# Transform writes issued from the scalar queue, a down projection of 512 and 128 columns, and a new order of all steps

## The chip, the cores and the metric

The kernel runs on one core of one Trainium2 chip. The core has TensorE (PE, matmuls), VectorE (DVE), ScalarE (ACT), GpSimd (POOL) and SyncE (SP, which here only issues DMAs). The metric is the device time of one execution in microseconds; several executions are made, and their median is compared.

## The reference

Two branches work on one layer-normed input of 2048 positions and 640 channels, and are added to the raw input:

```python
xn = layernorm(A_q)                              # over the 640 channels
ks = sum over 4 taps of shift_k * shifted A_k     # a short causal convolution
kv = ks * A_v
y  = irfft(rfft(kv, 4096) * rfft(ssm_k, 4096))[:2048]   # a long causal convolution, per channel
A  = xn * (y + kv * ssm_D)
B  = (sigmoid(xn @ w_gate) * (xn @ w_up)) @ w_down      # 640 -> 1728 -> 640
out = A_q + A + B
```

All tensors are bf16.

## The kernel before

The 2048 positions lie on 128 partitions with 16 blocks (b) each, so x and xn are tiles of 128 x 16 x 640. Branch B runs in four row groups t of four blocks. For each of 13 pieces fc of 128 hidden columns, `gate_mm` and `up_mm` (lines 295 and 302) make five matmuls of 512 columns each into a PSUM tile, ScalarE takes the sigmoid (`gate_ev`, line 298) and VectorE the product (`up_ev`, line 305); the last 64 columns of both share one product (`both_mm`, line 308). Then the down projection (`down_mm`, line 329) makes for each block bb two halves of 320 output columns, 14 matmuls each, in two parts of seven; only the last block of all is cut into 512 and 128. `down_ev` (line 338) adds a half to x on VectorE.

Branch A works in five chunks c of 128 channels. VectorE makes kv out of four taps in 16 operations (`kv_op`, line 356) and turns the long kernel around (`h_turn`, line 350). The long convolution is a transform in two stages, each a set of matmuls. `st1_mm` (line 386, step a) makes eight pairs of matmuls per chunk; `st1_ev` (step A) casts each pair out of PSUM into a tile t1, of which there are two, so that a tile holds two casts; `wr1` (line 404, step w, four per chunk) writes a tile of 512 KB to DRAM (d1), and `rd2` (line 412, step r) reads it back with the axes turned, for `st2_mm` (line 420, step b). After the product in frequency space (`prod`, step p), the inverse goes the same way: `inv1_mm` (line 445, step c, numbered y from 0 to 9), casts (`inv1_ev`, step C), `wr2` (line 468, step W, one or two DMAs by y), `rdb` (line 478, step R), `inv2_mm` (line 489, step d), and VectorE multiplies by xn and adds to x (step q).

PSUM is held by two pools: psC, two buffers of two banks, for the transform's first three matmul stages, and psG, four buffers of one bank, for the products, the down projection and the second inverse stage.

Casts are done by ScalarE, or by VectorE where the order has the letters F, J or I in place of B, C or A. In the kernel before every load, write and store of DRAM is issued by SP, but for three pieces of x at the start and the last store, which ScalarE issues. The normed rows are turned by DMA transposes (`xn_turn`, line 270, step e), also on SP.

The order is written out by hand as a string of letters, `ORDER` (line 671). Each letter takes the next step of its chain (`step`, line 562); chains m (early loads) and o (stores, line 342) are taken in the permuted sequence of `TURNS`. A letter fixes the place of its step on its own engine's queue; between engines only data and buffers order the work.

```python
    for k in "".join(ORDER.split()):
        fn, args = next(left[{"F": "B", "J": "C", "I": "A", "Y": "E"}.get(k, k)])
        fn(*args, **({"copy": dve_copy} if k in "FJIY" else {}))
```

Of the kernel before, what the change touches and what calls it, by code (L numbers as in the profile page):

```python
# [11 lines left out]
F32 = mybir.dt.float32  # L12
U16 = mybir.dt.uint16
ACT = mybir.ActivationFunctionType
ALU = mybir.AluOpType

S = 2048
DM = 640
FF = 1728
P = 128  # L20
NB = S // P
NC = DM // P
NFC = 14
# [42 lines left out]
def kernel(  # L66
# [14 lines left out]
    nc = tc.nc  # L81
# [19 lines left out]
    psG = ctx.enter_context(tc.tile_pool(name="psG", bufs=4, space=bass.MemoryType.PSUM))  # L101
# [14 lines left out]
    x = res.tile([P, NB, DM], BF16, name="x")  # L116
# [4 lines left out]
    wd = res.tile([P, NFC, DM], BF16, name="wd")  # L121
    hT = res.tile([P, NFC, 512], BF16, name="hT")
# [9 lines left out]
    sync = nc.sync  # L132
# [189 lines left out]

    pds = {}

    def cols(t, bb, half):
        m = 4 * P if (t, bb) == (3, 3) else DM // 2
        return slice(m, DM) if half else slice(0, m)

    def down_mm(t, bb, half, part):
        es = cols(t, bb, half)  # L330
        if part == 0:
            pds[bb, half] = psG.tile([P, es.stop - es.start], F32, name="pd", tag="g")
        pd = pds[bb, half]
        for fc in range(7 * part, 7 * part + 7):
            nc.tensor.matmul(pd[:, :], lhsT=hT[:, fc, bb * P:(bb + 1) * P], rhs=wd[:, fc, es],  # L335
                             start=(fc == 0), stop=(fc == NFC - 1))

    def down_ev(t, bb, half):
        es = cols(t, bb, half)
        nc.vector.tensor_tensor(x[:, 4 * t + bb, es], pds[bb, half][:, :], x[:, 4 * t + bb, es], ALU.add)  # L340

    def store(b0, b1, lo, hi):
        (nc.scalar if b1 == NB and hi == DM else sync).dma_start(outr[:, b0:b1, lo:hi], x[:, b0:b1, lo:hi])
# [60 lines left out]
    def wr1(c, k):  # L404
        h, part = divmod(k, 2)
        d = chunks[c]
        sync.dma_start(d["d1"][:, h, 8 * part:8 * part + 8, :], d[k].rearrange("p b s c -> p b (s c)"))

    groups = {}
    xz = cv.tile([P, 3, 3, 8, P], BF16, name="xz")  # L410
# [57 lines left out]
    def wr2(y):  # L468
        c, y2 = divmod(y, 2)
        d = chunks[c]  # L470
        if 2 * y % 3 < 2:
            sync.dma_start(d["d2"][16 * y2:16 * y2 + 16].rearrange("r p c -> p r c"), d["ao", y])
            return
        for n in range(2):
            lo = 16 * y2 + 8 - 8 * n
            sync.dma_start(d["d2"][lo:lo + 8].rearrange("r p c -> p r c"), d["ao", y][:, 8 * n:8 * n + 8, :])

    def rdb(c, n):

# [82 lines left out]
    def step(k, fn, *args):  # L562
        chains[k].append((fn, args))

    for t in range(4):
        for fc in range(0 if t else 2, 13):
            step("g", gate_mm, t, fc)
            step("s", gate_ev, t, fc)
            step("g", up_mm, t, fc)
            step("u", up_ev, t, fc)  # L570
        step("g", both_mm, t)
        step("s", both_ev, t)
        step("u", both_mul, t)
        firsts = [(0, 0, 0), (0, 1, 0), (0, 0, 1), (0, 1, 1)]
        for bb, e, part in firsts + [(k // 2, k % 2, n) for k in range(2, 8) for n in range(2)]:
            step("g", down_mm, t, bb, e, part)
            if part:
                step("u", down_ev, t, bb, e)

    def hs(c):  # L580
        return [(load_h, c)]
# [33 lines left out]
    for c in range(NC):  # L615
# [6 lines left out]
        for n in range(4):  # L622
            step("w", wr1, c, n)
# [7 lines left out]
        for y in (2 * c, 2 * c + 1):  # L631
            step("c", inv1_mm, y)
            for n in range(2):
                step("C", inv1_ev, y, n)
            step("W", wr2, y)
# [23 lines left out]
        for i in range(4):  # L659
            step("e", xn_turn, g, i)  # L660

    for b in range(0, 12, 2):
        step("o", store, b, b + 2, 0, 4 * P)
    for b in (0, 4, 8):
        step("o", store, b, b + 4, 4 * P, DM)
    for b in range(12, NB - 1):
        step("o", store, b, b + 1, 0, DM)
    step("o", store, NB - 1, NB, 0, 4 * P)
    step("o", store, NB - 1, NB, 4 * P, DM)

    ORDER = """
    mgmLggmmmssugmLuggsmZgmusmmgggmgmuLkHHLgsuksmkggsgmmmuusPlllmmggguklTkkkskkmugsgkumkgsgkmugggsumgKgn
    ekktDauAgakgguIgggLHkeauaggekAuugmDLLkwkeImuguTaaAkkmAgggkHuLwsaaPAgAgggkkkkakuKamkkkwsuggsghwkkAAsK
    aatAugVAuwkkggsHHkarasgukgAAasuggaDwkAAggKTKVsbkkuskkkwBlkggkFKaaAVugkskkpggrAktuusbgkwFBsguhpmuwaAa
    AHDgglsllaanpkkVwuAgsAggreakugpIwagkLkkekgAuuckkTkggCCaAggbBBggarwKkkkukkAKggtHeuubFrBegLuugpbFgBgaa
    kukkpkAAsggVWgkawakskApuugghHaAwDLrrwgspsIaAKugguLVcJCsggpubFpBkggWsbuggpsBuBaAgsakAPnggkspppuucCCgg
    sgrbrkHkglRskkwWBBruugdpbrkgspuBBlgsqdqwcCJqgugsRbBFWggbBBeeuggdkapqlrruqquaAAggldpwqaaAAqegpgagappg
    gIApcuggRJCuuuwebFBwggbuWBppgdquBpgdrrcJsCggqqRbWuFBsppprggsbBguBgsrducqqqdqggRCCbrppBggFubsgguppdBB
    ssqpqcWCdpgrugqqCsqbBFRguugbBBggdssppcgpqdugpqrqCCWusbFBppgWgsguugRcJsguCgsuggggqdduuqqqgguRddqqqgqq
    ggWRRgguuoddogoooqoqqudqdoggoqqoqqooouogguo  # L680
    """
    TURNS = {"m": [18, 21, 0, 5, 1, 10, 2, 7, 4, 14, 9, 6, 15, 12, 13, 11, 8, 17, 16, 20, 23, 22, 25, 24, 26, 19, 3],
        "o": [2, 0, 5, 3, 1, 4, 7, 6, 8, 9, 11, 10, 12, 13]}
    left = {k: iter([v[i] for i in TURNS.get(k, range(len(v)))]) for k, v in chains.items()}
    for k in "".join(ORDER.split()):
        fn, args = next(left[{"F": "B", "J": "C", "I": "A", "Y": "E"}.get(k, k)])
# [32 lines left out]
```

## Time and profile before

| what | value |
|---|---|
| median of 3 runs | 235.99 us (235.92 to 236.65) |
| the profiled execution, its own time | 236.99 us |
| its span in the profile | 234.9 us |
| DMA packets and bytes | 97760, 56.07 MB, mean 239 GB/s |
| DMA by queue | SP's 55.35 MB, ScalarE's 0.36 MB |
| landing of wr1's writes (d<-t), median | 5.7 us |
| landing of rd2's reads (t<-d), median | 6.0 us |

The profile comes from one execution. In a row of the timeline stand the start and the duration in us, the engine, the line of the kernel, the operation with its output and input, the count, and in brackets how long the engine stood idle before it and what released it. Durations of matmuls overlap, since they are pipelined; the pace is read from one start to the next. In a row of a stretch stand for each engine its busy time and its instructions.

### The profile page before, as it was taken

To read this page: it belongs to the slowest core of one execution; us is meant where nothing else is said; L and a number is where in the kernel's file an instruction comes from. 1 tells how busy PE (TensorE), PEld (TensorE's weight loads), DVE (VectorE), ACT (ScalarE), POOL (GpSimd) and SP (SyncE) were. 2 spreads that over 40 slices of the span, in tenths; PEclk is the share of its full clock that TensorE was granted. 3 is DMA by queue.
4 is the path that set the end of the run, shared out by engine and by line. 5 is a ranking of instruction groups with operands and counts; after the bars stand their busy time and mean duration, and the time that the engine had idled before them with its cause. 6 is when DMAs were issued, how large, how long until landed. Compare 5 with 4: busy or idle time off the path is not lost.

```text
span 234.9 us, 5606 instructions
## 1 busy us (share of the span) xinstructions
PE 227.9 (97%) x2281; PEld 121.9 (52%) x2281; DVE 203.0 (86%) x332; ACT 133.7 (57%) x193; POOL 13.1 (6%) x27
## 2 busy tenths in 40 slices
PE   7999999999999999999999999999899989999994
PEld 2854445665444444666444435476554444447772
DVE  4634899878989999999999999996999999995864
ACT  2477432279766587667687768563466656851000
POOL 5201300101100000000012000000000000000000
PEclk9999999999999999999999999999999999999999
DMA  6997999899998998999997998969999678583485
GB/s 174 325 264 158 293 316 252 168 267 209 314 301 204 257 318 275 213 252 180 290 308 180 305 288 192 307 125 279 317 243 265 184 180 226 139 247 104 140 309 178
DMA packets 97760, 56.07 MB, mean 239 GB/s; under 512 B 55943, under 2 KB 91975, under 8 KB 97607
## 3 DMA queue, kind: packets, MB, share of 16 engines
q1 hardware_dynamic: 97158, 55.35, 90.7%
q10 hardware_dynamic: 576, 0.36, 0.8%
q8 instruction: 18, 0.29, 0.6%
q14 instruction: 8, 0.06, 0.1%
HBM read 35.39 MB, written 18.35 MB: 229 GB/s over the span
## 4 chain that ended last, share of the span: by engine, by line
PE 42%; DVE 9%; DMA 5%; SPq 3%; issue 2%; ACT 1%; DVEq 0%
PE pu L291 11%; PE pd L335 11%; PE pg L291 10%; PE psb L495 3%; DMA d<-t 3%; DMA t<-d 2%; PE ps L427 2%; DVE hT L306 2%; PE psa L456 2%; SPq L271 2%; DVE xz L442 2%; DVE xz L440 1%; PE pg L312 1%; PE ps L395 1%; PE ps L393 1%
## 5 line engine op out<-in xcount | busy, mean ns | idle before, releaser
L291 PEld LDWEIGHTS <-w 128*128 128x128 bf16 x500 | 47.0, 98 | 58.4 <-issue 4.6
L335 PE MATMUL pd<-wd,hT 128*128 128x320 bf16 (+2 forms) x448 | 65.5, 299 | 0.0
L291 PE MATMUL pg<-xnT,w 128*128 128x512 bf16 x250 | 62.1, 379 | 0.3 <-ACT xn L223 0.3
L291 PE MATMUL pu<-xnT,w 128*128 128x512 bf16 x250 | 62.3, 380 | 0.0
L335 PEld LDWEIGHTS <-hT 128*128 128x128 bf16 x448 | 42.3, 98 | 21.3 <-issue 2.0
L254 ACT CAST t<-ps 128x1024 bf16<-128x1024 f32 x35 | 34.4, 1013 | 17.1 <-PE ps L395 11.5
L300 ACT ACTIVATE sig<-pg 128x512 bf16<-128x512 f32 x52 | 30.8, 600 | 23.1 <-PE pg L291 18.5
L306 DVE TENSOR_TENSOR hT<-sig,pu 128x512 bf16<-128x512 bf16 x52 | 34.5, 680 | 10.5 <-PE pu L291 5.7
L254 ACT CAST xz<-ps 128x1024 bf16<-128x1024 f32 x29 | 28.4, 1014 | 13.3 <-PE ps L427 13.2
L442 DVE TENSOR_TENSOR xz<-xz 128x2048 bf16<-128x2048 bf16 x20 | 24.4, 1220 | 0.3
L374 DVE TENSOR_TENSOR acc<-acc,tmp 128x1024 bf16<-128x1024 bf16 x30 | 20.7, 690 | 0.5
L372 DVE TENSOR_TENSOR tmp<-kx,sc 128x1024 bf16<-128x1024 bf16 x30 | 20.6, 686 | 0.4
L340 DVE TENSOR_TENSOR x<-pd,x 128x320 bf16<-128x320 f32 (+2 forms) x32 | 15.1, 484 | 5.0 <-PE pd L335 4.6
L500 DVE TENSOR_TENSOR yx<-psb,xn 128x512 bf16<-128x512 f32 x20 | 13.8, 690 | 2.4 <-PE psb L495 1.3
L395 PE MATMUL ps<-kvh,S1t 128*128 128x512 bf16 x40 | 15.5, 388 | 0.0
L393 PE MATMUL ps<-kvh,S1t 128*128 128x512 bf16 x40 | 15.1, 379 | 0.0
L254 ACT CAST ao<-psa 128x1024 bf16<-128x1024 f32 x12 | 11.8, 1014 | 5.5 <-PE psa L456 5.4
L440 DVE STREAM_SHUFFLE xz<-xz 128x512 f32<-128x512 f32 x20 | 14.5, 724 | 0.0
L257 DVE CAST xz<-ps 128x1024 bf16<-128x1024 f32 x11 | 13.4, 1219 | 0.3 <-PE ps L427 0.2
L495 PEld LDWEIGHTS <-TBt 128*128 128x128 bf16 x160 | 10.1, 98 | 2.9 <-issue 0.8
L223 ACT ACTIVATE xn<-x 128x640 bf16<-128x640 bf16 x12 | 8.8, 735 | 4.7 <-DMA x<-in_A_q_dram 4.7
L354 DVE STREAM_TRANSPOSE kvh<-hn 128x512 f32<-128x512 f32 x10 | 10.8, 1093 | 0.2 <-DMA hn<-in_A_ssm_k_dram 0.2
(54 smaller groups left out, 158.6 us busy)
## 6 DMA issues: line engine op xcount, KB each, us to landing
d<-t SPq DMA_DIRECT2D x20, 512.0 KB, 5.7
t<-d SPq DMA_DIRECT2D x20, 512.0 KB, 6.0
bi<-d SPq DMA_DIRECT2D x8, 512.0 KB, 5.2
d<-ao SPq DMA_DIRECT2D x6, 512.0 KB, 4.1
kx<-in_A_k_dram SPq DMA_DIRECT2D x10, 256.0 KB, 6.0
hn<-in_A_ssm_k_dram SPq DMA_DIRECT2D x20, 128.0 KB, 5.2
kvh<-in_A_v_dram SPq DMA_DIRECT2D x10, 256.0 KB, 6.2
x<-in_A_q_dram SPq DMA_DIRECT2D x3, 640.0 KB, 4.8
```

The lines of the kernel that those rows point to most:

```text
L254: nc.scalar.copy(out=out, in_=in_)
L291: nc.tensor.matmul(pg[:, :], lhsT=w[:, c, u * UP + fc * P:u * UP + (fc + 1) * P], rhs=xnT[:, :, c, :], start=(c == 0), stop=(c == NC - 1))
L300: nc.scalar.activation(sig[fc][:, :], pgs[0, fc][:, :], ACT.Sigmoid)
L306: nc.vector.tensor_tensor(hT[:, fc, :], sig[fc][:, :], pgs[1, fc][:, :], ALU.mult)
L335: nc.tensor.matmul(pd[:, :], lhsT=hT[:, fc, bb * P:(bb + 1) * P], rhs=wd[:, fc, es], start=(fc == 0), stop=(fc == NFC - 1))
L372: nc.vector.tensor_tensor(d["tmp"][:, :, :], kx[:, lo + 3 - m:hi + 3 - m, :], sb(m), ALU.mult)
L374: nc.vector.tensor_tensor(d["acc"][:, :, :], d["acc"][:, :, :], d["tmp"][:, :, :], ALU.add)
L393: nc.tensor.matmul(ps[:, 0, :, :], lhsT=S1[:, h, :], rhs=cin[c]["kvh"][:, 0, 4 * n4:4 * n4 + 4, :], start=True, stop=True)
L395: nc.tensor.matmul(ps[:, 1, :, :], lhsT=S1[:, h, :], rhs=hp[:, 2 * n4:2 * n4 + 2, :, :], start=True, stop=True)
L440: nc.vector.stream_shuffle(z[:, 2, :, :].bitcast(F32), z[:, 1, :, :].bitcast(F32), swap)
L442: nc.vector.tensor_tensor(z[:, 1:3, :, :], z[:, 0:1, :, :].to_broadcast((P, 2, 8, P)), z[:, 1:3, :, :], ALU.mult)
L495: nc.tensor.matmul(ps[:, i, :], lhsT=TB[:, h, 4 * m + i, :], rhs=bi[:, h, 4 * (m % 2) + i, :], start=(h == 0), stop=(h == 1))
```

## The change

- `wr1` and `wr2` issue their DMAs from ScalarE's queue in place of SP's.
- The down projection of a block makes 14 matmuls of 512 columns (`down_mm`), and its last 128 columns follow in a function of their own (`rest_mm`), with the rests of four blocks side by side in one PSUM tile; one VectorE addition (`rest_ev`) adds them to x. In the last row group the rests are kept as three and one.
- The stores of the rows 12 to 14, each of 640 columns, are cut into 512 columns and a joint piece of 128.
- `ORDER` and `TURNS` are new throughout.

```diff
--- before.py
+++ after.py
@@ -322,22 +322,27 @@
 
     pds = {}
 
-    def cols(t, bb, half):
-        m = 4 * P if (t, bb) == (3, 3) else DM // 2
-        return slice(m, DM) if half else slice(0, m)
-
-    def down_mm(t, bb, half, part):
-        es = cols(t, bb, half)
+    def down_mm(t, bb, part):
         if part == 0:
-            pds[bb, half] = psG.tile([P, es.stop - es.start], F32, name="pd", tag="g")
-        pd = pds[bb, half]
+            pds[bb] = psG.tile([P, 4 * P], F32, name="pd", tag="g")
         for fc in range(7 * part, 7 * part + 7):
-            nc.tensor.matmul(pd[:, :], lhsT=hT[:, fc, bb * P:(bb + 1) * P], rhs=wd[:, fc, es],
+            nc.tensor.matmul(pds[bb][:, :], lhsT=hT[:, fc, bb * P:(bb + 1) * P], rhs=wd[:, fc, 0:4 * P],
                              start=(fc == 0), stop=(fc == NFC - 1))
 
-    def down_ev(t, bb, half):
-        es = cols(t, bb, half)
-        nc.vector.tensor_tensor(x[:, 4 * t + bb, es], pds[bb, half][:, :], x[:, 4 * t + bb, es], ALU.add)
+    def down_ev(t, bb):
+        b = 4 * t + bb
+        nc.vector.tensor_tensor(x[:, b, 0:4 * P], pds[bb][:, :], x[:, b, 0:4 * P], ALU.add)
+
+    def rest_mm(t, bb, b0):
+        if bb == b0:
+            pds[t, b0] = psG.tile([P, 4, P], F32, name="pr", tag="g")
+        for fc in range(NFC):
+            nc.tensor.matmul(pds[t, b0][:, bb, :], lhsT=hT[:, fc, bb * P:(bb + 1) * P], rhs=wd[:, fc, 4 * P:DM],
+                             start=(fc == 0), stop=(fc == NFC - 1))
+
+    def rest_ev(t, b0, b1):
+        xs = x[:, 4 * t + b0:4 * t + b1, 4 * P:DM]
+        nc.vector.tensor_tensor(xs, pds[t, b0][:, b0:b1, :], xs, ALU.add)
 
     def store(b0, b1, lo, hi):
         (nc.scalar if b1 == NB and hi == DM else sync).dma_start(outr[:, b0:b1, lo:hi], x[:, b0:b1, lo:hi])
@@ -404,7 +409,7 @@
     def wr1(c, k):
         h, part = divmod(k, 2)
         d = chunks[c]
-        sync.dma_start(d["d1"][:, h, 8 * part:8 * part + 8, :], d[k].rearrange("p b s c -> p b (s c)"))
+        nc.scalar.dma_start(d["d1"][:, h, 8 * part:8 * part + 8, :], d[k].rearrange("p b s c -> p b (s c)"))
 
     groups = {}
     xz = cv.tile([P, 3, 3, 8, P], BF16, name="xz")
@@ -469,11 +474,11 @@
         c, y2 = divmod(y, 2)
         d = chunks[c]
         if 2 * y % 3 < 2:
-            sync.dma_start(d["d2"][16 * y2:16 * y2 + 16].rearrange("r p c -> p r c"), d["ao", y])
+            nc.scalar.dma_start(d["d2"][16 * y2:16 * y2 + 16].rearrange("r p c -> p r c"), d["ao", y])
             return
         for n in range(2):
             lo = 16 * y2 + 8 - 8 * n
-            sync.dma_start(d["d2"][lo:lo + 8].rearrange("r p c -> p r c"), d["ao", y][:, 8 * n:8 * n + 8, :])
+            nc.scalar.dma_start(d["d2"][lo:lo + 8].rearrange("r p c -> p r c"), d["ao", y][:, 8 * n:8 * n + 8, :])
 
     def rdb(c, n):
 
@@ -571,11 +576,19 @@
         step("g", both_mm, t)
         step("s", both_ev, t)
         step("u", both_mul, t)
-        firsts = [(0, 0, 0), (0, 1, 0), (0, 0, 1), (0, 1, 1)]
-        for bb, e, part in firsts + [(k // 2, k % 2, n) for k in range(2, 8) for n in range(2)]:
-            step("g", down_mm, t, bb, e, part)
+        for bb, part in ((0, 0), (1, 0), (0, 1), (1, 1), (2, 0), (2, 1)):
+            step("g", down_mm, t, bb, part)
             if part:
-                step("u", down_ev, t, bb, e)
+                step("u", down_ev, t, bb)
+        last = [(0, 3), (3, 4)] if t == 3 else [(0, 4)]
+        for b0, b1 in last:
+            if b1 == 4:
+                step("g", down_mm, t, 3, 0)
+                step("g", down_mm, t, 3, 1)
+                step("u", down_ev, t, 3)
+            for bb in range(b0, b1):
+                step("g", rest_mm, t, bb, b0)
+            step("u", rest_ev, t, b0, b1)
 
     def hs(c):
         return [(load_h, c)]
@@ -659,28 +672,27 @@
         for i in range(4):
             step("e", xn_turn, g, i)
 
-    for b in range(0, 12, 2):
+    for b in range(0, 14, 2):
         step("o", store, b, b + 2, 0, 4 * P)
-    for b in (0, 4, 8):
-        step("o", store, b, b + 4, 4 * P, DM)
-    for b in range(12, NB - 1):
-        step("o", store, b, b + 1, 0, DM)
+    step("o", store, 14, 15, 0, 4 * P)
+    for b in (0, 4, 8, 12):
+        step("o", store, b, min(b + 4, 15), 4 * P, DM)
     step("o", store, NB - 1, NB, 0, 4 * P)
     step("o", store, NB - 1, NB, 4 * P, DM)
 
     ORDER = """
-    mgmLggmmmssugmLuggsmZgmusmmgggmgmuLkHHLgsuksmkggsgmmmuusPlllmmggguklTkkkskkmugsgkumkgsgkmugggsumgKgn
-    ekktDauAgakgguIgggLHkeauaggekAuugmDLLkwkeImuguTaaAkkmAgggkHuLwsaaPAgAgggkkkkakuKamkkkwsuggsghwkkAAsK
-    aatAugVAuwkkggsHHkarasgukgAAasuggaDwkAAggKTKVsbkkuskkkwBlkggkFKaaAVugkskkpggrAktuusbgkwFBsguhpmuwaAa
-    AHDgglsllaanpkkVwuAgsAggreakugpIwagkLkkekgAuuckkTkggCCaAggbBBggarwKkkkukkAKggtHeuubFrBegLuugpbFgBgaa
-    kukkpkAAsggVWgkawakskApuugghHaAwDLrrwgspsIaAKugguLVcJCsggpubFpBkggWsbuggpsBuBaAgsakAPnggkspppuucCCgg
-    sgrbrkHkglRskkwWBBruugdpbrkgspuBBlgsqdqwcCJqgugsRbBFWggbBBeeuggdkapqlrruqquaAAggldpwqaaAAqegpgagappg
-    gIApcuggRJCuuuwebFBwggbuWBppgdquBpgdrrcJsCggqqRbWuFBsppprggsbBguBgsrducqqqdqggRCCbrppBggFubsgguppdBB
-    ssqpqcWCdpgrugqqCsqbBFRguugbBBggdssppcgpqdugpqrqCCWusbFBppgWgsguugRcJsguCgsuggggqdduuqqqgguRddqqqgqq
-    ggWRRgguuoddogoooqoqqudqdoggoqqoqqooouogguo
+    mLmgmggssmumggsgmLLmmmumugmmsHmmgggusugsLgmugmHgggZkkmPskmuggsgsusgkkkukmggglmlksemTmDauukkknAllsuka
+    AkkktggwkgggeeaHamguueIAkkkuTgaLAmakkggwKILguakKLaHkDkmwgguggLPAAkkVkgswggsgkkkhuusatKKAaggkkAkmkkks
+    waaluTkAAuwgrsrkggsHguaAgDakkkgkKAHVgausnkkawgmullAAsgbkktBFwuksggahaIsggpAwuukkkbBpBgsgusVaagglkkgu
+    rAAwskkpkgHasALeuueaKgapAAHggwkcCJgbDBuFkgaarATAVrgaeukgwALkkekbBKpkkFkwggubBFgtLggruaKKhAaAwgggpsaa
+    ppppkuWuksgVrAAwgLagPsAukkaAHllkwgggcsVgusgCCugHWbsrukDgBsgkkFbBBggusaanAkkgukggkAkppspcuRJsgruCgWbr
+    suFgpBpggswbgBuudprBdRgqqqscCCulkggskqpWlbgFuBeedbrrBkFgaadqppgAAepaIawAgcuCCpgqupgauRWIaAegwbrqqgdd
+    gFBRbgupprBqqgBpgcsCqqguuwgpCWgbFgdBpqsprsbugBBrgsqudRcCqggJbupBFpggWbssrBBggrupqpddscRuCqqqqCWggupb
+    BggFpppssubBguBgdrcCdCsqqggppbqRRFgsguBppggscuudgWgsCJWqqqguodqsuRggdqqqdqRgguuguogodqqqdgogoddqqgoo
+    qqoqqugoooouoguo
     """
-    TURNS = {"m": [18, 21, 0, 5, 1, 10, 2, 7, 4, 14, 9, 6, 15, 12, 13, 11, 8, 17, 16, 20, 23, 22, 25, 24, 26, 19, 3],
-        "o": [2, 0, 5, 3, 1, 4, 7, 6, 8, 9, 11, 10, 12, 13]}
+    TURNS = {"m": [21, 1, 18, 7, 0, 4, 6, 5, 9, 14, 2, 10, 13, 12, 15, 8, 20, 11, 17, 16, 22, 23, 25, 24, 26, 19, 3],
+        "o": [0, 4, 5, 1, 2, 9, 8, 7, 6, 10, 11, 3, 12, 13]}
     left = {k: iter([v[i] for i in TURNS.get(k, range(len(v)))]) for k, v in chains.items()}
     for k in "".join(ORDER.split()):
         fn, args = next(left[{"F": "B", "J": "C", "I": "A", "Y": "E"}.get(k, k)])
```

## The prediction

> **What bounds the kernel now.** I read the page's head first, then busy time by stretches, then TensorE's instructions in order of time, and last the waits and the chain of waits. The head and the stretches:
>
> ```profile
> span 234.9 us, 5606 instructions
> PE 227.9 (97%) x2281; PEld 121.9 (52%) x2281; DVE 203.0 (86%) x332; ACT 133.7 (57%) x193; POOL 13.1 (6%) x27
> ```
>
> ```profile
> 80.00:100.00 20.00, 20.00 (x167) 10.14 (x166) 19.73 (x31) 13.72 (x20) 0.48 (x1) 1.00 1.01 259
> 100.00:120.00 20.00, 19.91 (x210) 11.20 (x209) 19.66 (x33) 14.41 (x20) 0.00 (x0) 1.00 1.10 245
> 120.00:140.00 20.00, 20.00 (x212) 8.40 (x210) 19.97 (x30) 16.18 (x26) 2.46 (x3) 1.00 0.97 277
> 160.00:170.00 10.00, 9.23 (x122) 5.83 (x121) 7.71 (x12) 3.83 (x4) 0.00 (x0) 1.00 1.09 294
> 180.00:193.00 13.00, 12.08 (x202) 5.91 (x192) 12.65 (x22) 9.07 (x12) 0.00 (x0) 1.00 0.75 200
> ```
>
> The columns are PE, weight load, DVE, ACT and POOL busy, clock, DMA share, GB/s. TensorE and VectorE are both full from 80 us on, with one hole at 160 to 170, and the clock is full. So the kernel sits at TensorE's own work, VectorE right behind it, and an order can win only TensorE's gaps. These I take from starts in TensorE's timeline, since the printed ends overlap the next start:
>
> ```profile
> 20.33 1.24 PE L291 MATMUL pu<-xnT,w 128*128 128x512 bf16 x5
> 21.86 1.25 PE L291 MATMUL pg<-xnT,w 128*128 128x512 bf16 x5 [0.29 <-ACT xn L223]
> ...
> 162.85 2.06 PE L335 MATMUL pd<-wd,hT 128*128 128x320 bf16 x14
> 165.68 0.65 PE L456 MATMUL psa<-xz,SMt 32*32 32x512 bf16 x32 [0.77 <-DVE t L257]
> ...
> 187.64 1.03 PE L291 MATMUL pg<-xnT,w 128*128 128x512 bf16 x4
> 188.59 0.44 PE L427 MATMUL ps<-t,FWt 32*32 32x256 bf16 x32
> 188.97 1.25 PE L291 MATMUL pu<-xnT,w 128*128 128x512 bf16 x5
> 190.05 1.24 PE L291 MATMUL pg<-xnT,w 128*128 128x512 bf16 x5
> 191.13 0.61 PE L495 MATMUL psb<-bi,TBt 128*128 128x128 bf16 x8
> 192.66 0.65 PE L456 MATMUL psa<-xz,SMt 32*32 32x512 bf16 x32 [0.92 <-DVE xz L440]
> ```
>
> Five matmuls of 512 columns take 1.08 us (188.97 to 190.05), 0.216 each. So the first gap is 21.86 - 20.33 - 1.08 = 0.45 us. Fourteen of 320 columns take 1.90 (rows further below), so the second is 165.68 - 162.85 - 1.90 = 0.93. A matmul of 128 columns takes 0.056 (16 in 1.06 us, below, against 8 in 0.61), so eight take 0.44 and the third is 1.53 - 0.44 = 1.09. A step of 32-row matmuls starts some 0.09 late even where nothing waits (188.59 - 187.64 - 4 x 0.216), so 0.84 and 1.00 of the last two can go: **2.29 us in all**.
>
> The chain of waits and the list of waits name the causes:
>
> ```profile
> 155.64 0.46 ACT t L254
> ...
> 156.55 1.03 ACT t L254
> 157.59 6.62 DMA d<-t
> ...
> 164.41 1.24 DVE t L257
> ```
>
> ```profile
> DVE t L257 <- DMA d<-t: 2.3, 1, 2.3
> PEld L291 <- DMA w<-in_B_w_gate_dram: 0.8, 1, 0.8
> ```
>
> The reader is to see that the write of line 407 leaves SP right after its cast ends (157.58), and lands 6.62 us later. VectorE stands 2.3 us for its buffer (there are two tiles t1), TensorE follows at 165.68, and VectorE, which has no slack after that, hands the rest on as the gap at 192.66. The gap at 21.86 is put down to ScalarE; the weight load's wait names the real one, a piece of w.
>
> **The down projection: nothing on TensorE, little on VectorE.**
>
> ```profile
> 212.50 3.97 PE L335 MATMUL pd<-wd,hT 128*128 128x320 bf16 x28
> 216.30 1.06 PE L495 MATMUL psb<-bi,TBt 128*128 128x128 bf16 x16
> ...
> 227.48 3.97 PE L335 MATMUL pd<-wd,hT 128*128 128x512 bf16 x28
> ```
>
> Two halves of 320 take 3.80 us to the next start (0.136 each). The last row is the one block that already runs 14 of 512 and 14 of 128 columns: the same 3.97. So 0 us, in 16 blocks. On VectorE:
>
> ```profile
> L340 DVE TENSOR_TENSOR x<-pd,x 128x320 bf16<-128x320 f32 x30 | 14.1, 483 | 4.8 <-PE pd L335 4.6
> L340 DVE TENSOR_TENSOR x<-pd,x 128x512 bf16<-128x512 f32 x1 | 0.7, 691 | 0.1
> L257 DVE CAST xz<-ps 128x1024 bf16<-128x1024 f32 x11 | 13.4, 1219 | 0.3 <-PE ps L427 0.2
> ```
>
> Eight evictions of 483 become five of 512 elements at 691: 3.86 against 3.46, 0.41 less per row group, 1.2 in the three that lie before 193 us. The new order turns one more cast over to VectorE before its last inverse stage 1 (21 against 20): 1.22 back. VectorE's sum up to there is unchanged.
>
> **The order around t1.** The late write is chunk 4's second of four (wr1 4,1). Between the matmuls of step a whose cast it follows (4,3) and those whose cast needs its buffer (4,6) the old order has four down parts of 0.95, one inverse block of 0.44 and two a's of 0.43: 5.1 us of TensorE work. The new one has four parts of 7 x 0.216 = 1.51, one inverse block, one inverse stage 1 of 0.65 (the row at 192.66) and two a's: 8.0 us. That is 2.9 more, which covers VectorE's 2.3 us even if the write lands no sooner. Both gaps, 0.84 + 1.00, go. Without that cover the 2.3 us come back.
>
> **The order at the start.** In chain m the gate's piece of columns 768 to 1024 moves from the ninth place to the sixth, with 1664 KB of pieces ahead of it in place of 2368. At the rate of the third slice (264 GB/s, next row) 0.72 MB is 2.7 us, against a gap of 0.45: it goes. What moves back (kx, hn and the taps of chunk 0) is wanted behind the eviction of up's piece 7, which TensorE ends near 25.7 us (20.33 + 5 x 1.08). Up to kx's first half that is 5.7 MB from the start, which the slices of 5.87 us below reach near 24.5 us: 1 us of cover, more with the transposition of hn that VectorE does before.
>
> ```profile
> GB/s 174 325 264 158 293 316 252 168 267 209 314 301 204 257 318 275 213 252 180 290 308 180 305 288 192 307 125 279 317 243 265 184 180 226 139 247 104 140 309 178
> ```
>
> **The writes on ScalarE.** How long SP and ScalarE's queue hold an issue (ns, least, median, most; then start and us):
>
> ```profile
> L407 SPq DMA_DIRECT2D d<-t x20: 320/641/3037, 49.1 to 165.7; - x20
> ...
> DMA to landing us min/median/max: 4.0/5.7/7.0
> ```
>
> ```profile
> L472 SPq DMA_DIRECT2D d<-ao x6: 359/364/1377, 108.8 to 204.4; - x6
> ...
> L476 SPq DMA_DIRECT2D d<-ao x4: 367/472/584, 127.0 to 168.8; - x4
> ```
>
> ```profile
> 1.63 0.45 ACTq L512 DMA_DIRECT2D x<-in_A_q_dram  x1
> ...
> 231.81 0.35 ACTq L343 DMA_DIRECT2D out_dram<-x  x1
> ```
>
> 33 issues move: 20 of wr1, and of the ten wr2 seven with one piece and three with two. SP loses them; it waits less. ScalarE gains them, each behind a wait for its own or VectorE's casts, and what queues behind is the next cast or sigmoid, for which TensorE waits as psC has two buffers. From below an issue costs 0.35 (ScalarE's own rows), from above 3.04 (SP's worst); I take 0.40, since its own queue holds little else. 33 x 0.40 = 13 us on an engine with 16.18 busy of 20 in its fullest stretch; there four issues add 1.6. The cover at a reuse of psC is read here:
>
> ```profile
> 108.79 2.08 PE L335 MATMUL pd<-wd,hT 128*128 128x320 bf16 x14
> 109.02 1.01 ACT L254 CAST xz<-ps 128x1024 bf16<-128x1024 f32 x1 [0.81 <-PE ps L427]
> 109.55 1.22 DVE L257 CAST xz<-ps 128x1024 bf16<-128x1024 f32 x1
> 110.96 0.44 PE L427 MATMUL ps<-t,FWt 32*32 32x256 bf16 x32
> ```
>
> A cast starts 0.23 after the steps before it end, and TensorE follows it by 0.19. With 1.90 us of matmuls between, a ScalarE cast leaves 0.47, more than 0.40: hidden, 0 us. The 0.27 lost here (2.17 less 1.90) is VectorE arriving late. The new parts of 512 columns leave 1.51 where two parts of 320 left 1.90. A VectorE cast then needs 0.23 + 1.22 + 0.19 = 1.64: at least 0.13 over, and 0.27 + 0.39 = 0.66 where it comes late as here. The new order has two such places, inverse stage 1 of y = 0 and group 13. I take 0.3 each: **0.6 us given back** (0.3 to 1.3).
>
> **Stores.** 13 on SP and one on ScalarE, as before; the last two and the matmuls before them are the same. 0 us; one more piece in front of the end could cost the mean issue, some 0.5.
>
> **Sum.** 0.45 + 0.84 + 1.00 - 0.6 = 1.7 us, so the span 234.9 becomes 233.2. The profiled execution took 236.99, 2.1 around its span; the median of the runs, 235.99, is 1.0 below it. The forecast is 235.99 - 1.7 = 234.3, and its own range 233.7 (nothing given back) to 235.0 (1.3 given back).
>
> **Rivals.** *ScalarE holds the evictions: slower.* In the new order 15 of the 33 writes have a psC cast as ScalarE's next instruction. Past 0.47 us an issue is paid by TensorE. The gain is used up when 15 x (i - 0.47) = 1.7, at i = 0.58 us, and SP's median for line 407 is already 0.64. With one in twenty at SP's worst, 3.04, the mean is 0.64 + 2.4 / 20 = 0.76; that is 15 x 0.29 = 4.3 us, and 234.3 + 4.3 = 238.6. For it: DMA shares of about 1.0 up to 140 us. Against: ScalarE's own rows, 0.35 to 0.45, and a ring that holds one or two writes where SP's holds loads and transposes too.
>
> *The write still lands too late: no change.* If landing grows from 6.6 to over 9 us, the 2.9 us of new cover are gone, VectorE stands 2.3 us again, and 0.45 - 0.6 is left: 236.1. The profile has 7.0 as its longest, which speaks against it; a DMA share of 1.09 at that place speaks for it. The Trainium skill speaks against the change here (DMA: Bandwidth & Descriptors, "Issuing engines are not separate DMA queues"): DMAs of the scalar and sync engines run on the same 16 DMA engines, and a second issuer saves only issue time. The row at 157.59 agrees that issue time was not what was late. By the rule alone the landing stays at 6.6 to 7.0 and comes 0.4 later by ScalarE's issue behind its casts, which leaves 0.2 of VectorE's wait at most: 234.5, an estimate.
>
> **How the numbers follow.** A measurement of this kernel can tell 0.3%, 0.7 us, from no change. The forecast gets 0.53, the held evictions 0.30, the late landing 0.17. So faster by over 0.7 us 0.53, within 0.17, slower 0.30. The range reaches down to 233.0, 0.7 under the forecast's own, for late starts that I do not count, with a tenth left below, and up to 238.6, the slower rival's price, which leaves a tenth above.
>
> **What would show it.** Right: no wait of a t cast for d<-t; TensorE's start-to-start gaps near 21, 165 and 192 us gone; VectorE over 9.5 of 10 busy in 160 to 170; ScalarE's issues at 0.35 to 0.5 us; matmuls of 128 columns at 0.056. Wrong: ScalarE issues of 0.6 us and more with psC casts late behind them, TensorE idle before lines 393, 427 or 456 in 80 to 180 us, or VectorE waits for kx, kvh or hn before 60 us.

## The result, and the profile after

| | before | after |
|---|---|---|
| median, same chip | 236.06 us (6 runs, 235.6 to 236.65) | 238.53 us (6 runs, 237.4 to 240.48) |
| the profiled execution | 236.99 us, span 234.9 | 239.68 us, span 237.9 |
| last matmul's end, then to the end of the span | 231.45, 3.4 us | 233.22, 4.7 us |

The changed kernel is slower: ratio 1.0105, 95% interval 1.0065 to 1.0144, 2.5 us where the forecast said 1.7 us less. Its runs also spread over 3 us, three times as far as those of before. The medians here and below are of all runs, while a ratio leaves out the runs that took over 1.5% longer than the fastest of their kernel.

The head of the page, and busy time by the stretches that the prediction showed:

```profile
span 237.9 us, 5583 instructions
PE 226.9 (95%) x2268; PEld 113.2 (48%) x2281; DVE 203.2 (85%) x322; ACT 132.6 (56%) x192; POOL 12.2 (5%) x27
```

```profile
80.00:100.00 20.00, 18.79 (x115) 8.29 (x115) 18.86 (x29) 13.95 (x20) 0.42 (x1) 1.00 0.81 214
...
120.00:140.00 20.00, 19.44 (x178) 8.33 (x177) 18.14 (x28) 15.00 (x22) 1.60 (x3) 1.00 0.90 266
160.00:170.00 10.00, 9.84 (x80) 4.34 (x78) 9.47 (x14) 5.34 (x6) 0.00 (x0) 1.00 1.03 271
180.00:193.00 13.00, 13.00 (x222) 6.01 (x221) 12.16 (x21) 9.13 (x12) 0.00 (x0) 1.00 0.84 227
```

Read against before: the hole at 160 to 170 is filled (TensorE 9.84 for 9.23), that at 180 to 193 too (13.00 for 12.08), but 80 to 100 and 120 to 140, which were full, have lost 1.2 and 0.6 us. TensorE's timeline, at the places of the three old gaps (21, 164 and 194 us) and at the new ones:

```profile
20.21 1.24 PE L291 MATMUL pu<-xnT,w 128*128 128x512 bf16 x5
21.29 1.24 PE L291 MATMUL pg<-xnT,w 128*128 128x512 bf16 x5
...
39.65 1.89 PE L329 MATMUL pd<-wd,hT 128*128 128x512 bf16 x8
42.38 4.69 PE L329 MATMUL pd<-wd,hT 128*128 128x512 bf16 x21 [0.84 <-DMA wd<-in_B_w_down_dram]
...
82.85 1.24 PE L291 MATMUL pu<-xnT,w 128*128 128x512 bf16 x5
85.25 1.24 PE L291 MATMUL pg<-xnT,w 128*128 128x512 bf16 x5 [1.16 <-ACT sig L300]
...
126.91 0.96 PE L461 MATMUL psa<-xz,SMt 32*32 32x512 bf16 x32
128.43 1.24 PE L291 MATMUL pu<-xnT,w 128*128 128x512 bf16 x5 [0.56 <-DVE hT L306]
...
162.54 1.67 PE L329 MATMUL pd<-wd,hT 128*128 128x512 bf16 x7
164.14 0.65 PE L461 MATMUL psa<-xz,SMt 32*32 32x512 bf16 x32
...
193.31 1.06 PE L500 MATMUL psb<-bi,TBt 128*128 128x128 bf16 x16
194.29 0.65 PE L461 MATMUL psa<-xz,SMt 32*32 32x512 bf16 x32
...
206.14 0.44 PE L432 MATMUL ps<-t,FWt 32*32 32x256 bf16 x32
207.12 1.24 PE L291 MATMUL pu<-xnT,w 128*128 128x512 bf16 x5 [0.54 <-DVE yx L505]
232.28 0.94 PE L340 MATMUL pr<-wd,hT 128*128 128x128 bf16 x14
```

Start to start less the matmuls' pace, as in the prediction: 21.29 follows 20.21 by 1.08, 164.14 follows 162.54 by 1.60 (seven of 0.216 are 1.51) and 194.29 follows 193.31 by 0.98 (sixteen of 0.056 are 0.90), so the old gaps are gone. New ones stand at 42.38 (2.73 - 8 x 0.216 = 1.0 us, the second half of wd is late), 85.25 (2.40 - 1.08 = 1.3, a sigmoid of ScalarE), 128.43 (1.52 - 0.58 = 0.9, VectorE) and 207.12 (0.98 - 0.37 = 0.6, an eviction of VectorE): 3.8 us against the 2.3 taken away. The end, from the last matmul on, has grown by 1.2. A cast of t still waits once for d<-t, 0.8 us, and VectorE is busy 9.47 of 10 in 160 to 170, just under the 9.5 that the prediction named.

What the moved writes took of ScalarE's queue (ns, least, median, most), and how long they took to land:

```profile
L412 ACTq DMA_DIRECT2D d<-t x20: 326/327/1940, 47.4 to 177.1; - x20
...
DMA to landing us min/median/max: 2.7/4.6/8.0
```

An issue is cheap, 0.33 us in the median and 0.45 in the mean of all 33 moved writes, two of which were held: one of d1 for 1.94 us, one of d2 (line 481) for 1.50. What is dear is seen in ScalarE's timeline at the two gaps (an ACTq row is the issue of a DMA):

```profile
80.71 1.00 ACT L254 CAST xz<-ps 128x1024 bf16<-128x1024 f32 x1
84.23 0.33 ACTq L412 DMA_DIRECT2D d<-t  x1
84.60 1.08 ACT L300 ACTIVATE sig<-pg 128x512 bf16<-128x512 f32 x2 [2.89 <-DMA x<-in_A_q_dram]
...
117.66 0.42 ACTq L477 DMA_DIRECT2D d<-ao  x1
...
121.10 1.94 ACTq L412 DMA_DIRECT2D d<-t  x1
123.09 0.74 ACT L223 ACTIVATE xn<-x 128x640 bf16<-128x640 bf16 x1 [2.02 <-issue]
```

At 81.71 ScalarE is done with its cast, but stands 2.89 us until a load of x has landed. The sigmoid does not read x. The instruction ahead of it is the write wr1(1,3), and the built program lets it wait for the completion counter that this load raised last: the DMAs of both queues share eight such counters in turn, so a DMA waits for the one numbered eight before it. On SP such a wait delays other DMAs; on ScalarE it delays casts and sigmoids. At 121.10 the issue itself is held for 1.94 us; the LayerNorm of group 3 behind it is late, then GpSimd's power, for which VectorE stands 1.66 us, and VectorE's `xn`, and TensorE stands at 128.43.

### The profile page after: what moved, and what is told of

The parts are those of the page before. It is cut to its first block, busy times and chain, and to the rows that moved or that the text cites. A ratio compares the mean times of both kernels' runs of the same rounds, so it can differ in the third digit from the quotient of the medians.

```text
span 237.9 us, 5583 instructions
## 1 busy us (share of the span) xinstructions
PE 226.9 (95%) x2268; PEld 113.2 (48%) x2281; DVE 203.2 (85%) x322; ACT 132.6 (56%) x192; POOL 12.2 (5%) x27
## 4 chain that ended last, share of the span: by engine, by line
PE 62%; DVE 15%; DMA 14%; issue 4%; SPq 3%; POOL 1%; ACT 0%; ACTq 0%; DVEq 0%; POOLq 0%
PE pd L329 16%; PE pu L291 14%; PE pg L291 13%; DMA wd<-in_B_w_down_dram 4%; DMA x<-in_A_q_dram 4%; DMA kvh<-in_A_v_dram 4%; PE psb L500 3%; PE pr L340 3%; PE ps L432 3%; PE psa L461 2%; PE ps L400 2%; PE ps L398 2%; DVE acc L379 2%; DVE tmp L377 2%; DVE xz L447 1%
## 5 line engine op out<-in xcount | busy, mean ns | idle before, releaser
L329 PE MATMUL pd<-wd,hT 128*128 128x512 bf16 x213 | 50.7, 379 | 1.7 <-DMA wd<-in_B_w_down_dram 0.8
L254 ACT CAST xz<-ps 128x1024 bf16<-128x1024 f32 x27 | 26.6, 1013 | 14.0 <-PE ps L432 14.0
L329 PEld LDWEIGHTS <-hT 128*128 128x128 bf16 x224 | 21.2, 98 | 26.7 <-issue 2.6
L257 DVE CAST xz<-ps 128x1024 bf16<-128x1024 f32 x13 | 15.8, 1219 | 1.2 <-PE ps L432 1.1
L254 ACT CAST ao<-psa 128x1024 bf16<-128x1024 f32 x13 | 12.7, 1015 | 5.3 <-PE psa L461 5.3
L400 PE MATMUL ps<-kvh,S1t 128*128 128x512 bf16 x40 | 15.5, 387 | 0.1
L398 PE MATMUL ps<-kvh,S1t 128*128 128x512 bf16 x38 | 14.4, 378 | 0.0
L340 PE MATMUL pr<-wd,hT 128*128 128x128 bf16 x224 | 14.2, 219 | 0.0
L340 PEld LDWEIGHTS <-hT 128*128 128x128 bf16 x224 | 13.0, 98 | 1.7 <-issue 0.5
L334 DVE TENSOR_TENSOR x<-pd,x 128x512 bf16<-128x512 f32 x16 | 10.8, 684 | 2.3 <-PE pd L329 2.2
```

Of the source, the lines that this page charges most:

```text
L254: nc.scalar.copy(out=out, in_=in_)
L257: nc.vector.tensor_copy(out, in_)
L329: nc.tensor.matmul(pds[bb][:, :], lhsT=hT[:, fc, bb * P:(bb + 1) * P], rhs=wd[:, fc, 0:4 * P], start=(fc == 0), stop=(fc == NFC - 1))
L340: nc.tensor.matmul(pds[t, b0][:, bb, :], lhsT=hT[:, fc, bb * P:(bb + 1) * P], rhs=wd[:, fc, 4 * P:DM], start=(fc == 0), stop=(fc == NFC - 1))
L398: nc.tensor.matmul(ps[:, 0, :, :], lhsT=S1[:, h, :], rhs=cin[c]["kvh"][:, 0, 4 * n4:4 * n4 + 4, :], start=True, stop=True)
L400: nc.tensor.matmul(ps[:, 1, :, :], lhsT=S1[:, h, :], rhs=hp[:, 2 * n4:2 * n4 + 2, :, :], start=True, stop=True)
```

## The experiments

All were measured beside the kernel before on the same chip, in 6 or more runs. A difference between two of them is that of their ratios, times 236 us; each ratio's interval reaches 0.2 to 0.5% to either side, 0.5 to 1.1 us, so the smaller differences count only where two pairs or the profiles agree.

### Who issues the writes

The changed kernel with SP issuing all 33 writes again:

```diff
-        nc.scalar.dma_start(d["d1"][:, h, 8 * part:8 * part + 8, :], d[k].rearrange("p b s c -> p b (s c)"))
+        sync.dma_start(d["d1"][:, h, 8 * part:8 * part + 8, :], d[k].rearrange("p b s c -> p b (s c)"))
...
-            nc.scalar.dma_start(d["d2"][16 * y2:16 * y2 + 16].rearrange("r p c -> p r c"), d["ao", y])
+            sync.dma_start(d["d2"][16 * y2:16 * y2 + 16].rearrange("r p c -> p r c"), d["ao", y])
...
```

> The changed kernel with the 33 writes of lines 412, 477 and 481 issued by SyncE again, its new order, its down projection and its stores kept. Theory A (the writes cost the time through what they wait for on ScalarE's queue, so that casts and sigmoids stand behind them): the gaps of TensorE at 85.25 (1.32 us) and 128.43 us (0.94 us) go, those at 42.38 us (1.0 us, the second half of wd) and at the end (1.24 us after the last matmul) stay, so 238.5 - 2.2 = 236.3 us. Theory B (the new order is the slower one, whoever issues the writes): 238.5 us or more, with gaps of the same sum.

Measured 236.63 us, ratio 1.0032 (1.0008 to 1.0056). The gaps at 85 and 128 are gone, wd's is 0.5 us, the end 3.9 us. Theory A holds: the issuer is worth 1.7 us of the loss (give or take 1.1), and the rest, 0.75 us, is the order's own. Wd's smaller gap is not the issuer's doing, since the first moved write leaves only at 44.2 us here and at 47.4 in the changed kernel, both behind that gap.

The reverse, the kernel before with only the issuer changed (the same lines 407, 472 and 476, `sync` to `nc.scalar`):

> The kernel before, in its old order, with only the 33 writes of lines 407, 472 and 476 issued by ScalarE. Theory A (waits of the writes on ScalarE's queue hold its casts): slower than 236.0 us by 2 to 6 us, with gaps of TensorE behind ScalarE's casts and sigmoids. Theory B (the writes' issuer costs nothing, the new order does): 235 to 236 us, since the landing falls from 5.7 to about 4.6 us and the VectorE wait of 2.3 us for d<-t goes.

Measured 258.42 us, ratio 1.0954 (1.0915 to 1.0993): not 2 to 6 but 22.5 us. The old order cannot bear it at all. Its list of waits (us in total, times, longest):

```profile
ACT t L254 <- DMA d<-t: 26.1, 7, 7.0
```

Then one kind of write at a time. First the changed kernel with d2 on SP, d1 on ScalarE, beside the changed kernel unaltered:

> The changed kernel with only the 13 writes of d2 (lines 477 and 481) issued by SyncE again; those of d1 (line 412) stay on ScalarE. If ScalarE's issue of 1.94 us at 121.10 was held because d2 writes with many rows stood in its own queue, the hold and TensorE's gap at 128.43 us (0.94 us) go: 237.5 us. If any write behind ScalarE's casts costs the same, it stays within 0.5 us of 238.5 us.

> The changed kernel once more, unaltered, beside the three kernels below and the kernel before, for the spread of its gaps between profiles. If the gaps of TensorE at 42, 85 and 128 us and the end come from its order and its queues, they are there again with sizes within about 0.5 us, and the median is near 238.5 us, 1.0105 of before; if they are chance, other gaps stand in their place and the median still is the same.

Measured 237.83 us, ratio 1.0074 (1.0046 to 1.0103), and unaltered 239.06 us, 1.0134 (1.0091 to 1.0176): 1.4 us for the d2 writes, give or take 1.2. Without them no issue of d1 is held:

```profile
L412 ACTq DMA_DIRECT2D d<-t x20: 326/326/383, 48.4 to 176.3; - x20
```

and TensorE goes on from 126.93 to 127.52, without a gap (a step of these 32 matmuls takes 0.58). In all six profiles of the new order with d2 on ScalarE the d1 write some 3.5 us behind the first d2 write was held 1.49 to 1.94 us; in both without, the longest issue was 0.38. The distance alone is not the cause. In the changed kernel another d1 write stands as far behind another d2 write and was not held:

```profile
143.20 0.37 ACTq L477 DMA_DIRECT2D d<-ao  x1
146.73 0.34 ACTq L412 DMA_DIRECT2D d<-t  x1
```

Nor is ScalarE's queue alone in being held there: an issue of SP, the load of kvh at 120.81, took 3.37 us, and with all d2 writes on SP the one at 117.70 took 3.32. And the gap behind the held issue, 0.5 to 0.9 us in these profiles, is less than the 1.4; what the rest is was not found. In the unaltered kernel's second profile the gaps at 43 (1.4 us), 127.6 (0.6) and 206 (0.6) are there again, that at 85 is not: ScalarE's wait for x was 1.5 us there, and hidden.

The same split in the old order, d1 alone on ScalarE:

> The kernel before, in its old order, with only the 20 writes of d1 issued by ScalarE, those of d2 by SyncE. Both kinds on ScalarE cost 22.5 us in this order. If the d1 writes behind ScalarE's own instructions, and the casts that wait for their buffers t1, make that loss: 250 us or more, with casts waiting for d<-t by some 15 us. If the d2 writes ahead of them in the queue make it, by holding the next issue (5.50 us at 125.54): below 245 us, without issues of d1 over 1 us.

Measured 252.15 us, ratio 1.0667 (1.062 to 1.0714): 15.7 of the 22.5 us come with the d1 writes, though no issue took over 0.38 us. ScalarE's timeline of this kernel shows how:

```profile
46.90 0.74 ACT L223 ACTIVATE xn<-x 128x640 bf16<-128x640 bf16 x1 [3.90 <-DMA x<-in_A_q_dram]
...
48.59 0.99 ACT L254 CAST t<-ps 128x1024 bf16<-128x1024 f32 x1
...
52.02 0.83 ACT L224 ACTIVATE xn<-x,lnq 128x640 bf16<-128x640 bf16 x1
52.08 0.33 ACTq L407 DMA_DIRECT2D d<-t  x1
...
58.06 1.93 ACT L254 CAST t<-ps 128x1024 bf16<-128x1024 f32 x2 [5.12 <-DMA d<-t]
...
60.80 0.33 ACTq L407 DMA_DIRECT2D d<-t  x1
```

The first write's two casts had ended by 44.6 us (VectorE's at 43.4 took 1.2). The write leaves at 52.08, behind the LayerNorm, which itself waited for x. Its buffer comes free at 58, and only then does the next cast of t run, for which TensorE stands 2.6 us. The second write, cast by 51.1, stands behind that very cast and leaves at 60.80. In the kernel before SP sent the first at 49.1, 4.0 us after its casts in place of 7.5. So the writes become late because they stand behind other work of ScalarE, and two buffers t1 cannot take that. A part of both losses is TensorE's clock, granted at 0.97 in the mean with all writes on ScalarE and 0.985 with d1 alone, as the last section shows.

### The wait for x

> The changed kernel with one step moved in the written order: the write wr1(1,2) is placed ahead of the load of x's third part on SyncE instead of behind it. No engine's own order of instructions changes, only the numbering of the DMAs among the eight completion semaphores that both queues share. Theory A (ScalarE's 2.9 us wait at 84.6 us is the write wr1(1,3) held until the load of x's last part, the DMA eight places earlier, has landed): that wait and TensorE's gap at 85.25 us (1.32 us) go, so about 237.2 us. Theory B (the gap comes from the casts or the loads themselves): 238.5 us, gap unchanged.

```diff
-    waaluTkAAuwgrsrkggsHguaAgDakkkgkKAHVgausnkkawgmullAAsgbkktBFwuksggahaIsggpAwuukkkbBpBgsgusVaagglkkgu
+    waaluTkAAuwgrsrkggsHguaAgDakkkgkKAHVgauswnkkagmullAAsgbkktBFwuksggahaIsggpAwuukkkbBpBgsgusVaagglkkgu
```

This one tells nothing of its question: in the built program the move changed no instruction, wait or number of a DMA, so the kernel is the changed one again. Measured 239.12 us, ratio 1.014 (1.0101 to 1.018), with wd's gap (1.4 us), a gap behind VectorE's product at 65.7 (1.4), and no wait for x, since ScalarE came late to that write. Its use is to show the spread: in one program, gaps of over 1 us, as this one at 65.7 and that at 85, come and go from profile to profile.

What does change the numbers is SP's own order, SMt ahead of x:

```diff
-    waaluTkAAuwgrsrkggsHguaAgDakkkgkKAHVgausnkkawgmullAAsgbkktBFwuksggahaIsggpAwuukkkbBpBgsgusVaagglkkgu
+    waaluTkAAuwgrsrkggsHguaAgDakkkgkKAHVgausmnkkawgullAAsgbkktBFwuksggahaIsggpAwuukkkbBpBgsgusVaagglkkgu
```

> The changed kernel with only SMt loaded ahead of the third part of x. If ScalarE's wait at 84 us (1.5 to 2.9 us in five profiles of this order, put down to the load of x) belongs to the write wr1(1,3), which by the program waits for the DMA numbered eight before it: it falls by 1.2 us or more, since SMt is issued 1.4 us earlier than x's issue ends and is small, and TensorE's gap at 85 us is at most 0.3 us; the median falls by 0 to 1.3 us against 238.5 to 239.1. If the wait belongs to the sigmoid or its data: unchanged.

Measured 238.59 us, ratio 1.0095 (1.0073 to 1.0116). ScalarE's timeline at the place:

```profile
81.46 1.00 ACT L254 CAST xz<-ps 128x1024 bf16<-128x1024 f32 x1
82.29 0.33 ACTq L412 DMA_DIRECT2D d<-t  x1
82.66 1.09 ACT L300 ACTIVATE sig<-pg 128x512 bf16<-128x512 f32 x2 [0.20 <-ACT xz L254]
```

The sigmoid follows 0.2 us behind the cast, where four of the five other profiles of this order show 1.5 to 2.9, and TensorE has no gap there. So the wait was the write's, for a load it has nothing to do with. In the median it is worth little: 0.7 us under the mean of the three ratios of the unaltered program (1.0126), which their intervals do not tell from nothing.

### The down projection alone

The kernel before with 512 and 128 columns in every block:

```diff
-        m = 4 * P if (t, bb) == (3, 3) else DM // 2
+        m = 4 * P
```

> The kernel before with its down projection in 512 and 128 columns for every block in place of 320 and 320, still half by half and with 8 evictions per row group (4 of 512, 4 of 128 columns); order and queues as before. Theory A (the columns cost nothing on TensorE, 3.97 us a block either way): within 0.7 us of 236.0. Theory C (pieces of 128 columns cost TensorE time of their own): slower by 1 us or more, with a longer step for the 128 column pieces than 14 x 0.056 = 0.78 us.

Measured 236.05 us, ratio 1.0013 (0.9996 to 1.0031). Theory A: the columns cost at most 0.7 us, and are not seen.

### Places in the new order

The lists of the loads at the start and of the stores:

```diff
-    TURNS = {"m": [21, 1, 18, 7, 0, 4, 6, 5, 9, 14, 2, 10, 13, 12, 15, 8, 20, 11, 17, 16, 22, 23, 25, 24, 26, 19, 3],
-        "o": [0, 4, 5, 1, 2, 9, 8, 7, 6, 10, 11, 3, 12, 13]}
+    TURNS = {"m": [21, 1, 18, 7, 0, 4, 6, 5, 9, 14, 2, 10, 13, 12, 15, 8, 11, 17, 20, 16, 22, 23, 25, 24, 26, 19, 3],
+        "o": [0, 4, 5, 1, 2, 3, 7, 6, 8, 9, 10, 11, 12, 13]}
```

> The changed kernel with two lists reordered: the second half of wd goes before the rest of kx and the second hn in the loads of the start, and the stores go in the order in which their rows are ready. If these two places are slower by their order alone: TensorE's gap near 42 us (1.0 us) goes and the time after the last matmul falls from 4.7 to about 3.6 us, so 238.5 - 2.1 = 236.4 us. If the wait for wd is set by the rate of all transfers, and the tail by the last store alone, nothing moves: 238.5 us.

> The changed kernel with all 33 writes issued by SyncE again and the two lists reordered as in the kernel above. If the three causes add (writes on ScalarE 1.7 us by the run of that alone, 236.6 us; wd about 0.5 us there; the tail about 0.7 us): 235.3 us, a little faster than before. If the new order is slower for another reason: 236.6 us.

With the writes on ScalarE 237.18 us over 12 runs, ratio 1.0026 (0.9997 to 1.0056) without the three longest of them: 1.9 us by the medians and 2.5 by the ratios under the unaltered kernel measured beside it. With them on SP 235.66 us, ratio 0.9968 (0.9945 to 0.9991), 1.5 us under the same kernel without the two lists. Wd's gap is gone from both profiles, and the last matmul is followed by 3.2 and 2.9 us. The last issue of a store on SP, in the changed kernel and then with the writes on SP and the lists mended:

```profile
L348 SPq DMA_DIRECT2D out_dram<-x x13: 372/462/1814, 215.2 to 234.1; - x13
```

```profile
L348 SPq DMA_DIRECT2D out_dram<-x x13: 344/377/1110, 213.6 to 231.7; - x13
```

The first leaves 0.9 us after the last matmul (233.22), behind stores whose rows had long been ready; the second just as the last matmul ends (231.70).

One step more, the eviction of VectorE at the gap near 206 us:

```diff
-    BggFpppssubBguBgdrcCdCsqqggppbqRRFgsguBppggscuudgWgsCJWqqqguodqsuRggdqqqdqRgguuguogodqqqdgogoddqqgoo
+    BggFpppssubBguBgdrcCdCsqqggqppbRRFgsguBppggscuudgWgsCJWqqqguodqsuRggdqqqdqRgguuguogodqqqdgogoddqqgoo
```

> All 33 writes on SyncE, the two lists reordered (wd earlier, stores by readiness), and one step of VectorE moved: the eviction of the inverse block (2,3) ahead of the product of group 18. If TensorE's gap of 0.6 us near 206 us, which every kernel in the new order showed (0.59 to 0.62), is this eviction standing behind the product's 2.0 us, it goes: 235.7 - 0.6 = 235.1 us, ratio 0.994. If VectorE only hands it on: 235.7 us, with a gap of that size a few steps later.

Measured 234.44 us, ratio 0.995 (0.9925 to 0.9976): faster than both kernels, 1.2 us under before. The difference to the kernel above, 0.4 us, is within the intervals, but in the profile the gap is gone and none has come behind it:

```profile
203.32 0.44 PE L432 MATMUL ps<-t,FWt 32*32 32x256 bf16 x32
203.69 1.25 PE L291 MATMUL pu<-xnT,w 128*128 128x512 bf16 x5
```

### The mended order with other issuers

From here on the order and lists are those of the last kernel. With d1 on ScalarE and SMt ahead of x:

> The kernel above with the 20 writes of d1 on ScalarE, and the small table SMt loaded ahead of the third part of x in place of behind it, so that the write wr1(1,3) waits for SMt. Theory A (what ScalarE's queue costs are the waits of single writes, and with the d2 writes and the wait for x away little is left): ScalarE's wait at 84 us falls below 1 us, and the time is within 0.7 us of the kernel above, 235.1 to 235.8 us. Theory B (each write on ScalarE costs, whatever it waits for): 1.0 us over the kernel above or more, as the kernel with only d1 on ScalarE stood 1.0 us over that with none.

Measured 234.75 us, ratio 0.9943 (0.992 to 0.9967): level with the kernel that has all on SP, to some 0.8 us. That is Theory A: a write on ScalarE is not dear as such. But its waits are not all gone. The first write of d1 leaves at 48.22 us, behind a copy of ScalarE that stands 7.2 us for the load of `sraw`, where SP sent it at 43.50; a cast of t then waits 0.77 us for d<-t, and TensorE for the cast:

```profile
54.38 0.38 PE L398 MATMUL ps<-kvh,S1t 128*128 128x512 bf16 x1 [0.29 <-ACT t L254]
```

This profile is of the longest of eight runs, 236.16 us.

With d2 on ScalarE as well:

> The changed kernel, all 33 writes on ScalarE as in the change, with the four lists mended: wd earlier, stores by readiness, SMt ahead of x's third part, the eviction of the inverse block (2,3) ahead of the product of group 18. It differs from the kernel with only d1 on ScalarE (0.9943 of before) by the 13 writes of d2 alone. If the d2 writes cost through the held issue near 121 us (1.5 to 1.9 us in five profiles) and the late LayerNorm behind it: 1.4 us over that kernel, 236.2 us, no faster than before, with TensorE's gap at 128 us of 0.5 to 0.9 us. If the earlier difference of 1.4 us came from elsewhere in the order: 234.8 us.

Measured 235.98 us, ratio 0.9996 (0.997 to 1.0022): the d2 writes cost 1.25 us here too, give or take 0.8, with the held issue (1.64 us at 121.24) and TensorE's gap at 128.26 (0.6 us) back. The profiled run is one of the two longest of twelve; its largest gap, 1.5 us at 55.48, stands behind a cast that waits for d<-t, long before the first d2 write at 117.79, and is not theirs.

With all 33 on GpSimd:

> The first kernel of this call with the 33 writes issued by GpSimd, which has little else to do (5% busy), in place of SyncE. If what a write waits for matters only through what stands behind it on its engine: 234.5 to 235.5 us, with no casts or sigmoids late. Rival: a write issued by GpSimd is dearer than the 0.33 us that ScalarE and SyncE take, or lands later than 5.7 us, so that buffers t1 come free late: 237 us or more.

Measured 236.52 us, ratio 1.001 (0.9984 to 1.0035), 1.4 us over SP: neither 234.5 to 235.5 nor 237. An issue is dearer there:

```profile
L412 POOL DMA_DIRECT2D d<-t x20: 533/549/782, 40.8 to 168.8; - x20
```

and the landings are longer than with all on SP (5.5 us for d<-t and 6.7 for t<-d, against 5.0 and 5.4). Which of the two makes the 1.4 us was not tried.

## Why the prediction was wrong

**The step that failed** is "its own queue holds little else ... hidden, 0 us" for the writes on ScalarE. It priced the issue, and that price was right: 0.33 us in the median and 0.45 in the mean for a forecast of 0.40. It names the waits in front of a write, "each behind a wait for its own or VectorE's casts", and the casts and sigmoids behind it, but puts no time on the waits; that a write also waits for the counter of a DMA it has nothing to do with, and that an issue can be held, are not in it. In the changed kernel's order the writes on ScalarE cost 1.7 us by the kernel with SP (1.0032 against 1.0105), 2.4 by the second measurement of the unaltered one (1.0134): 1.4 of it came with the d2 writes, where the held issue is the one cause seen, and the rest with d1. There the wait for x made a gap of 1.3 us in one profile, but its removal changed the median by no more than the noise; the late first write, behind the load of `sraw`, is another wait that the traces show without its price.

**The start** had a second hole. The working followed the gate's piece, kx, hn and the taps, and the gap at 21.86 did go, though in four other profiles of the new order TensorE waits 0.3 to 0.6 us for another piece of the gate near 30 us. It did not follow wd's second half, which the new list puts behind 512 KB more: 1.0 to 1.7 us of TensorE in the unaltered order, 0.5 with the writes on SP. **The stores** were put at 0 us with "some 0.5" for one more piece in front of the end; the end grew by 1.2 us in the profile. Wd and stores together are 1.5 us by the ratios with the writes on SP, 1.9 to 2.5 with them on ScalarE.

**The order's gaps were right.** "0.45 + 0.84 + 1.00" are gone, and with the causes above mended the new order is 1.2 us (0.995) or 1.3 us (0.9943) faster than before. That this lies inside the 1.0 to 2.3 of the forecast's own range is in part luck: about 0.6 of it stands behind the last matmul (2.9 us for 3.4 in the profiles), where the forecast expected nothing. Of the 0.6 us given back at two VectorE casts, the changed kernel shows no gap over 0.3 us; in the kernel with ratio 0.995 the first of the two places has one, 0.56 us by the starts, behind VectorE's cast of inverse stage 1, and the second has none:

```profile
100.18 0.28 PE L432 MATMUL ps<-t,FWt 32*32 32x256 bf16 x2
100.75 0.43 PE L432 MATMUL ps<-t,FWt 32*32 32x256 bf16 x30 [0.29 <-DVE ao L257]
```

In the changed kernel 0.6 us were lost instead where the eviction at 206 us stands behind a product, a place that the working never looked at. **The down projection's** 0 us holds by its own kernel (1.0013).

**The rivals.** The held evictions had the right engine and direction. That their price, 238.6 us, met the measured 238.53 is luck: it charges the writes 4.3 us by a mean over 15 issues, where 18 of the 20 of d1 took 0.33 to 0.34 us and the writes cost 1.7 to 2.4, and it holds none of the order's own 0.75 us. The mean of 0.58 us an issue at which the gain would be used up was not reached in the new order (0.45 at most); the loss came by a few single waits. The late landing did not come: 4.6 us for 5.7. Whether the second queue helped is not shown: in the unaltered order d<-t lands in 5.3 us with all writes on SP and in 4.6 with all on ScalarE, in the mended order in 5.0 on SP and in 5.4 with d1 on ScalarE. The Trainium skill (DMA: Bandwidth & Descriptors, "Issuing engines are not separate DMA queues") says that the DMAs of all issuing engines run on the same 16 DMA engines, and that a second issuer saves only issue time. These landings, once sooner and once later, do not speak against it, and the issue time saved was here outweighed by the waits that moved along.

Open stays why the write behind the first d2 write is held, how the whole 1.4 us of the d2 writes reach TensorE, and how the 1.0 us of the d1 writes in the unaltered order (1.0074 against 1.0032) divide between the wait for x, the late first write and others.

## What to carry to other kernels

When a DMA moves from an idle queue to a computing engine, price the wait in front of it and not the issue: list for each what it waits for, the completion counters it shares with other queues among them, and what stands behind it on the new engine. A queue that only issues DMAs delays no cast when it stands waiting, though it delays the DMAs behind; a write placed behind other work of an engine also frees its buffer later. And in a new order follow every load and store that changed its place, not only those that were late before.

## What the runs showed of the hardware

- TensorE's granted clock fell after a long stand. In the old order with all writes on ScalarE it stood 7.41 us, and the next five matmuls of 512 columns (140.54) took 2.13 us to the following start, where five take 1.08 at full speed; the granted clock was 0.73 in 140 to 145 us and 1.00 in 145 to 150:

```profile
131.08 1.24 PE L291 MATMUL pu<-xnT,w 128*128 128x512 bf16 x5 [0.81 <-DVE hT L306]
139.73 0.58 PE L393 MATMUL ps<-kvh,S1t 128*128 128x512 bf16 x1 [7.41 <-ACT t L254]
140.11 0.63 PE L395 MATMUL ps<-kvh,S1t 128*128 128x512 bf16 x1
140.54 2.30 PE L291 MATMUL pg<-xnT,w 128*128 128x512 bf16 x5
142.67 0.39 PE L393 MATMUL ps<-kvh,S1t 128*128 128x512 bf16 x1
```

  With d1 alone on ScalarE a stand of 2.48 us, at 59.12, was enough: the granted clock was 0.51 in 60.8 to 63.0 us, and five such matmuls took 2.13 there too. The gaps of the new order, up to 1.5 us of standing, left it at 1.00. So a long gap costs more than its length.
- The issue of a DMA can be held after its waits are over: on ScalarE the d1 write behind the first d2 write for 1.5 to 1.9 us, in six profiles of six, while another in the same place behind a later d2 write took 0.34.
- An issue by GpSimd took 0.55 us, one by ScalarE 0.33.
